# Joining float64 weights in two VectorE operations instead of three, and preparing the first weight earlier

## Chip, cores and metric

The kernel runs on one core of a Trainium2 chip. The metric is the device time of one execution in microseconds (us). Three executions of the kernel before took 1155.07, 1155.97 and 1156.25 us; the median is 1155.97 us.

## What is computed

Local attention, then a gated layer, then a second layer with SiLU; 3072 tokens, model width 512. All inputs arrive as float64 arrays for the weights and float32 for q, k and v (see `_layout`); the cut reference:

```python
# attention, chunks of 32 queries, window = 8 memory + 16 left + 32 + 8 right keys
scores = scale * q_c @ k_full.T
a = softmax(scores);  out[:, :, c] = a @ v_full
x = out.transpose(0, 2, 1, 3).reshape(3072, 512)
# first layer, d_ff 1536
x = (sigmoid(x @ w_gate) * (x @ w_val)) @ w_out
# second layer, d_ff 2048
h = x @ w_in
return (h * sigmoid(h)) @ w_out2
```

The weights are float64 on the device, seen as pairs of int32 words (low, high). The kernel makes a float32 of each, then splits that into two parts, a rounded one ("high part", fp32r) and the rest ("lower part"), and replaces each product by three matmuls: high x high, high x lower, lower x high.

## The kernel before

All engines run in an order written out by hand (`tc.manual_schedule()`); each engine takes its instructions in the order in which the program emits them, and waits where an input is not there.

**A weight unit** (class `Unit`, lines 96 to 135) is 128x512 float64 values, 512 KB, in a staging buffer `stg` (4 buffers). Its life has five steps: `load` (one DMA on SP's queue), `rebias` (ScalarE, L106: the high words, read as float32, times 2^-112, which moves the exponent's bias from double to single), `join` (VectorE, three operations: L114 shifts the low word right by 29, L117 ors the sign bit of the high word into it, L121 shifts the high word left by 3 and ors the low word to it, which gives the float32 `t`), `high` (ScalarE, L128: copy to fp32r), `rest` (VectorE, L131: `t` minus the high part). The class `Feed` moves three units at once: step k emits high of unit k-2, rebias of k, join of k-1, rest of k-2, and loads up to unit k+3.

**The first layer** takes the tokens in six blocks of 512 (index 0 to 5). In each block it goes over 12 slices f of the hidden width. A slice is 12 matmuls into `pg` (gate, L270), 12 into `pv` (value, L270) and 12 of the output product `y` of the slice before (L89, L91, L93), all 128x128 by 128x512. `pg` and `pv` share two PSUM banks, so the next `pv` waits until VectorE has multiplied this one (L285). After `pg` comes ScalarE's sigmoid (L280). In block 0 the three units of a slice are prepared on the way, one step of the feed after `pg`, one after `pv`, one after `y`: 36 units in all. In blocks 1 to 5 the first layer's weights are there, and the 32 units of the second layer pass through the same `rebias` and `join` (`prepare2`). The attention of the next block's four tiles of 128 tokens lies between: scores (L196, L209 to L211), normalising (L217 to L220), turning (L226, L227), product with v (L236, transposed by VectorE at L243).

**The start** (lines 400 to 431) computes the attention of block 0, four tiles in a pipeline, with idle transposes on TensorE (`warm`, L390). Unit 0 (the gate weight of slice 0) is rebiased and joined in the fifth round, its high part and the rebias of unit 1 (the value weight) are in the sixth. After the last tile's product, `split_x` makes the high and lower part of the four 128-row pieces of x (L81 on ScalarE, L84 on VectorE, or on GpSimd for the last NP pieces), then come the join of unit 1 and the rest of unit 0. The first `pg` of block 0 goes first over high and lower part of the weight with the high parts of x, and takes the four lower parts of x last; other slices of block 0 take the lower part of the weight last.

**The second layer** runs behind the first on prepared weights and its lines (L674, L787) are not touched.

Of the kernel before, what the change touches and what calls it, by code (L numbers as in the profile page):

```python
# [11 lines left out]
AF = mybir.ActivationFunctionType  # L12
ALU = mybir.AluOpType
# [21 lines left out]
LV = 1  # L35
NQ = ()
NJ = 8
NP = 2
NRING = 5

A11, S2, S1, S3, A12, A22, S4, A21 = range(8)
# [5 lines left out]
def moe_kernel(ctx: ExitStack, tc: tile.TileContext, qh, kh, vh, wg, wv, wo, w2i, w2o, out):  # L47
    nc = tc.nc
# [17 lines left out]
    def t_slot(name):  # L66
        return p1.tile([P, 512], F32, tag="t", name=name, bufs=2)
# [28 lines left out]
    class Unit:  # L96
# [5 lines left out]
            nc.sync.dma_start(out=self.stg.rearrange("p a b -> p (a b)"), in_=self.src)  # L102

        def rebias(self):
            high = self.stg[:, :, 1].bitcast(F32)
            nc.scalar.activation(out=high, in_=high, func=AF.Copy, scale=2.0**-112)  # L106

        def join(self, into=None):

            if into is None:  # L110
                self.t = t_slot(f"t_{self.name}")
                into = self.t
            low, high = self.stg[:, :, 0], self.stg[:, :, 1]
            nc.vector.tensor_scalar(  # L114
                out=low, in0=low, scalar1=29, scalar2=None, op0=ALU.logical_shift_right
            )
            nc.vector.scalar_tensor_tensor(  # L117
                out=low, in0=high, scalar=-2147483648, in1=low,
                op0=ALU.bitwise_and, op1=ALU.bitwise_or,
            )  # L120
            nc.vector.scalar_tensor_tensor(  # L121
                out=into.bitcast(I32), in0=high, scalar=3, in1=low,
                op0=ALU.logical_shift_left, op1=ALU.bitwise_or,
            )
# [63 lines left out]
    def att_scores(t, ps_sc, e):  # L188
        sc = ps_sc(f"sc{t}")
        scv = sc.rearrange("p (c2 a k) -> p c2 a k", c2=2, a=4)  # L190
        qb, kt = q_t.pop(t), k_t.pop(t)
        for c2 in range(2):
            for a in range(4):
                for cp in range(2):
                    c = 2 * c2 + cp
                    nc.tensor.matmul(  # L196
                        scv[cp * 64 : cp * 64 + 64, c2, a],
                        qb[:, 4 * a + c].rearrange("p u q -> p (u q)"),
                        kt[:, a, c],
                        start=True,  # L200
                        stop=True,
                    )
        if t % TPB == 0:
            nc.vector.memset(scv[0:64, 0, :, NMEM : NMEM + LEFT], NEG)
        if t % TPB == TPB - 1:
            nc.vector.memset(scv[64:128, 1, :, WIN - RIGHT : WIN], NEG)
        s3 = sc.rearrange("p (g k) -> p g k", k=WIN)
        m = att.tile([P, 8, 1], F32, tag="m", name=f"m{t}", bufs=2)
        nc.vector.tensor_reduce(m, s3, axis=AX.X, op=ALU.max)  # L209
        nc.vector.tensor_tensor(out=e, in0=s3, in1=m.to_broadcast([P, 8, WIN]), op=ALU.subtract)  # L210
        nc.scalar.activation(out=e, in_=e, func=AF.Exp, scale=SCALE)  # L211
        e_t[t] = e

    def att_norm(t, eng=nc.vector):
        e = e_t[t]
        r = att.tile([P, 8, 1], F32, tag="r", name=f"r{t}", bufs=2)
        nc.vector.tensor_reduce(r, e, axis=AX.X, op=ALU.add)  # L217
        nc.vector.tensor_scalar_add(r, r, 1e-9)
        nc.vector.reciprocal(r, r)
        eng.tensor_tensor(out=e, in0=e, in1=r.to_broadcast([P, 8, WIN]), op=ALU.mult)  # L220

    def att_turn(t, ps_pt, at):
        e = e_t.pop(t).rearrange("p g k -> p (g k)")
        pt = ps_pt(f"pt{t}")
        for i in range(4):
            nc.tensor.transpose(pt[:, i * P : (i + 1) * P], e[:, i * P : (i + 1) * P], ident)  # L226
        nc.scalar.copy(at.rearrange("p a b q -> p (a b q)"), pt)  # L227
        at_t[t] = at

    def att_pv(t, ps_px, xt, off):  # L230
        at, vb = at_t.pop(t), v_t.pop(t)
        px = ps_px(f"px{t}")
        for c in range(4):
            for j in range(4):
                q0 = 64 * (c % 2) + 32 * (j % 2)
                nc.tensor.matmul(  # L236
                    px[32 * j : 32 * j + 32, c * P : (c + 1) * P],
                    at[:, c // 2, j // 2, q0 : q0 + 32],
                    vb[c * len(vb) // 4][:, :, c % (4 // len(vb)), j],
                    start=True,  # L240
                    stop=True,
                )
        nc.vector.transpose(  # L243
            out=xt[:, :, off : off + P].rearrange("p k (c q) -> p c k q", c=4),
            in_=px.rearrange("p (c k q) -> p c k q", c=4, k=4),
        )
# [8 lines left out]
    def split_x(src, n, name, on_pool=0, hi_dve=()):  # L255
        xs = []
        for kt in range(KT):
            x = p1.tile([P, 2, 512], F32R, tag="x", name=f"{name}_{kt}", bufs=5)
            lo_eng = nc.gpsimd if kt >= KT - on_pool else nc.vector
            hi_eng = nc.vector if kt in hi_dve else nc.scalar  # L260
            split(x[:, 0, :n], x[:, 1, :n], src[:, kt, :n], lo_eng, hi_eng)
            xs.append(x)
        return xs
# [34 lines left out]
    with tc.manual_schedule():  # L298
# [57 lines left out]
        units = []  # L356
# [31 lines left out]
        def idle(n):  # L388
            for _ in range(n):
                nc.tensor.transpose(warm[:, :P], ident, ident)  # L390

        def prefetch(t):
            if t < NTILE:
                att_load_qk(t, qA, k_tile(t))

        def prefetch_v(t):
            if t < NTILE:
                att_load_v(t, vA)

        idle(22)  # L400
        for i in range(n0 + 2):
            if i < n0:
                att_scores(i, ps_y, es[i])
                idle(NI)
            if 0 <= i - 2 < n0:
                at = hold[0].tile([P, 512], F32, tag="sg", name=f"at{i - 2}", bufs=3)
                att_turn(i - 2, ps_a, at.rearrange("p (a b q) -> p a b q", a=2, b=2))
                idle(NI if i < 4 else 0)
            if 0 <= i - 1 < n0:
                att_norm(i - 1, nc.gpsimd if i - 1 in NQ else nc.vector)  # L410
            if 0 <= i - 3:
                att_pv(i - 3, ps_y, x32[0], (i - 3) * P)
                idle(NI if i < 4 else 0)
            if i == 1:
                prefetch(n0)
            if i == 4:
                prefetch_v(n0)
            if i == n0:
                units[0].rebias()
                units[0].join()  # L420
            if i == n0 + 1:
                units[0].high()
                units[1].rebias()
        att_pv(n0 - 1, ps_y, x32[0], (n0 - 1) * P)
        idle(NJ)
        x = split_x(x32.pop(0), BLOCKS1[0], "x0", NP, NH)
        units[1].join()
        units[0].rest()
        units[2].rebias()
        feed1.n = 3  # L430
        feed1.step()
# [525 lines left out]
```

## Time and profile before

| | |
|---|---|
| median of 3 runs (lowest, highest) | 1155.97 us (1155.07, 1156.25) |
| profiled execution: span, first to last instruction | 1153.2 us |
| what lies around the span, taken against the median | 2.8 us |
| TensorE matmul busy | 1133.1 us, 98% |
| VectorE busy | 685.9 us, 59%, 1013 instructions |
| ScalarE busy | 487.8 us, 42%, 708 instructions |
| GpSimd busy | 52.1 us, 5% |
| mean granted TensorE clock | 0.997 |

For the profiled execution the page gives the span and no other time; the 2.8 us is the median of the runs less the span. Starts are counted from the span's first instruction. A line of a timeline is one instruction, or several merged ones (x4). "Idle before" and the releaser behind an arrow say how long an engine had stood, and what ended it.

### The profile page before, as it was taken

Reading aid. Unit: us, or ns where it says so; the run is one execution under the profiler, and the core shown is the slowest. Engines: PE = TensorE matmul, PEld = TensorE weight load, DVE = VectorE, ACT = ScalarE, POOL = GpSimd, SP = SyncE. Lnnn points to the kernel's source line nnn. Section 1 sums busy time; section 2 is a strip of 40 time slices with the busy share of each in tenths; the row PEclk is TensorE's granted clock in tenths of the full one; section 3 lists DMA queues with packets and bytes.
Section 4 is the critical chain, followed back from the end, with each engine's and each line's share of the span. In section 5 each row is a group of like instructions: output and inputs, shape, how many; then the busy total and the mean of one; then the engine's idle time right before and its main releaser. Section 6 shows DMA issues by size and latency. Waiting matters only on the chain.

```text
span 1153.2 us, 15956 instructions
## 1 busy us (share of the span) xinstructions
PE 1133.1 (98%) x6319; PEld 926.5 (80%) x6319; DVE 685.9 (59%) x1013; ACT 487.8 (42%) x708; POOL 52.1 (5%) x46
## 2 busy tenths in 40 slices
PE   8899999999999999999999999999999999999998
PEld 6677788888888888888888888888888888888887
DVE  7899975455546555554545533348944379544665
ACT  3555643343334333433433324444434455344442
POOL 1000000000000000000000001111001110011000
PEclk9899999999999999999999999999999999999999
DMA  9787776667666566576565455575665575655552
GB/s 312 236 262 269 255 273 211 210 217 230 196 209 226 202 218 225 197 247 204 193 230 181 124 191 175 196 277 209 221 218 195 209 277 211 226 193 205 200 209 84
DMA packets 79210, 248.51 MB, mean 215 GB/s; under 512 B 7584, under 2 KB 23968, under 8 KB 69920
## 3 DMA queue, kind: packets, MB, share of 16 engines
q1 hardware_dynamic: 79136, 247.49, 63.2%
q8 instruction: 50, 0.82, 0.3%
q14 instruction: 24, 0.20, 0.1%
HBM read 199.23 MB, written 48.23 MB: 215 GB/s over the span
## 4 chain that ended last, share of the span: by engine, by line
PE 86%; DVE 9%; DMA 3%; issue 1%; ACT 1%; SPq 0%; DVEq 0%; ACTq 0%
PE o L787 20%; PE c L674 20%; PE pg L270 14%; PE pv L270 14%; PE y L89 5%; PE y L91 5%; PE y L93 5%; PE sc L196 2%; PE px L236 1%; DVE w L131 1%; DMA v<-in_vh_dram 1%; DVE stg_wv L117 1%; DVE sg L285 1%; PE pt L226 1%; DVE stg_wo L117 1%
## 5 line engine op out<-in xcount | busy, mean ns | idle before, releaser
L674 PE MATMUL c<-xp,wr 128*128 128x512 f32 x1008 | 229.1, 389 | 0.0
L787 PE MATMUL o<-gf,wr 128*128 128x512 f32 x1008 | 229.0, 389 | 0.0
L674 PEld LDWEIGHTS c<-xp,wr 128*128 128x128 f32 x1008 | 189.2, 188 | 39.3
L787 PEld LDWEIGHTS o<-gf,wr 128*128 128x128 f32 x1008 | 189.2, 188 | 39.3
L270 PE MATMUL pg<-x,w 128*128 128x512 f32 x864 | 211.8, 394 | 5.7 <-DVE w L131 5.2
L270 PE MATMUL pv<-x,w 128*128 128x512 f32 x864 | 211.2, 393 | 5.2 <-DVE sg L285 5.2
L270 PEld LDWEIGHTS pg<-x,w 128*128 128x128 f32 x864 | 162.3, 189 | 41.1 <-DVE w L131 5.6
L270 PEld LDWEIGHTS pv<-x,w 128*128 128x128 f32 x864 | 160.0, 188 | 41.9 <-issue 8.6
L84 DVE TENSOR_TENSOR gf<-g,gf 128x1024 fp32r<-128x1024 f32 x84 | 104.1, 1242 | 49.8 <-ACT gf L81 49.6
L81 ACT CAST gf<-g 128x1024 fp32r<-128x1024 f32 x84 | 88.3, 1055 | 86.7 <-PE o L787 71.4
L287 ACT CAST g<-sg 128x512 fp32r<-128x512 f32 x72 | 44.9, 623 | 156.1 <-DVE sg L285 156.1
L694 POOL TENSOR_TENSOR s<-s,s 128x512 f32<-128x512 f32 x24 | 36.0, 1498 | 943.6 <-ACT s L693 943.6
L290 DVE TENSOR_TENSOR g<-sg,g 128x512 fp32r<-128x512 f32 x72 | 49.8, 691 | 42.6 <-ACT g L287 42.6
L280 ACT ACTIVATE sg<-pg 128x512 f32<-128x512 f32 x72 | 43.0, 597 | 75.2 <-PE pg L270 62.0
L646 DVE TENSOR_TENSOR s<-c,s 128x512 f32<-128x512 f32 x48 | 33.2, 692 | 65.1 <-PE c L674 63.0
L89 PE MATMUL y<-g,wor 128*128 128x512 f32 x240 | 66.2, 397 | 0.5 <-DVE y L548 0.5
L91 PE MATMUL y<-g,wor 128*128 128x512 f32 x240 | 64.3, 390 | 0.0
L93 PE MATMUL y<-g,wor 128*128 128x512 f32 x240 | 64.1, 389 | 0.0
L285 DVE TENSOR_TENSOR sg<-pv,sg 128x512 f32<-128x512 f32 x72 | 49.4, 686 | 20.6 <-PE pv L270 20.5
L649 DVE TENSOR_TENSOR g<-g,g 128x1024 f32<-128x1024 f32 x48 | 58.6, 1220 | 0.0
L652 ACT ACTIVATE g<-s 128x512 f32<-128x512 f32 x48 | 30.4, 634 | 54.1 <-DVE s L646 54.1
L91 PEld LDWEIGHTS y<-g,wor 128*128 128x128 f32 x240 | 45.1, 188 | 9.6
(119 smaller groups left out, 1040.9 us busy)
## 6 DMA issues: line engine op xcount, KB each, us to landing
wr<-w2o_d SPq DMA_DIRECT2D x42, 1024.0 KB, 4.8
wor<-wo_d SPq DMA_DIRECT2D x60, 512.0 KB, 4.9
wr<-w2i_d SPq DMA_DIRECT2D x24, 1024.0 KB, 5.1
wr<-w2i_d SPq DMA_DIRECT2D x24, 768.0 KB, 4.4
w2o_d<-coo SPq DMA_DIRECT2D x56, 256.0 KB, 3.0
w2i_d<-coi SPq DMA_DIRECT2D x24, 512.0 KB, 3.0
qA<-in_qh_dram SPq DMA_DIRECT2D x21, 512.0 KB, 5.0
k<-in_kh_dram SPq DMA_DIRECT2D x21, 512.0 KB, 5.8
```

The lines of the kernel that those rows point to most:

```text
L81: nc.scalar.copy(hi, src)
L84: lo_eng.tensor_tensor(out=lo, in0=src, in1=hi.bitcast(F32), op=ALU.subtract)
L89: nc.tensor.matmul(o, w_hi, x_hi, start=first, stop=False)
L91: nc.tensor.matmul(o, w_hi, x_lo, start=False, stop=False)
L93: nc.tensor.matmul(o, w_lo, x_hi, start=False, stop=last)
L270: nc.tensor.matmul(o[:, :n], w[:, pw, kt * P : (kt + 1) * P], x[kt][:, px, :n], start=i == 0, stop=i == len(steps) - 1,)
L285: nc.vector.tensor_tensor(out=sg[:, :n], in0=psv[:, :n], in1=sg[:, :n], op=ALU.mult)
L287: nc.scalar.copy(g[:, 0, :n], sg[:, :n])
L290: nc.vector.tensor_tensor(out=g[:, 1, :n], in0=sg[:, :n], in1=g[:, 0, :n].bitcast(F32), op=ALU.subtract)
L649: nc.vector.tensor_tensor(out=o, in0=a, in1=b_, op=ALU.subtract)
L674: nc.tensor.matmul(o, w[:, pw, i % 4, kt * P : (kt + 1) * P], X[i][:, px, kt], start=first and j == 0, stop=j == 5, skip_group_check=not f ...
L787: nc.tensor.matmul(c[at[i], dp], w[:, pw, pl, dp * P : (dp + 1) * P], f[:, px, pl], start=i in (A11, S1, S2) and pp == 0 and j == 0, stop= ...
```

## The change

`rebias` uses the parametric ReLU with alpha 2^32 instead of a scaled copy. A positive word is multiplied by 2^-112 as before; a negative one by 2^-112 and 2^32. That adds 32 to the exponent field of negative words, which sets a bit that the shift by 3 in `join` carries to the sign position (the old sign bit is shifted out). So the operation that placed the sign (L117) is gone from `join`. NP goes from 2 to 0: GpSimd makes no lower part of x any more, VectorE makes all four. And in the sixth round of the start `rest` of unit 0 and `join` of unit 1 are emitted directly behind the rebias of unit 1, ahead of the last tile's product and `split_x`.

```diff
-NP = 2
+NP = 0
...
         def rebias(self):
+
             high = self.stg[:, :, 1].bitcast(F32)
-            nc.scalar.activation(out=high, in_=high, func=AF.Copy, scale=2.0**-112)
+            nc.scalar.activation(
+                out=high, in_=high, func=AF.Prelu, scale=2.0**-112, alpha=2.0**32
+            )
...
             nc.vector.tensor_scalar(
                 out=low, in0=low, scalar1=29, scalar2=None, op0=ALU.logical_shift_right
-            )
-            nc.vector.scalar_tensor_tensor(
-                out=low, in0=high, scalar=-2147483648, in1=low,
-                op0=ALU.bitwise_and, op1=ALU.bitwise_or,
             )
             nc.vector.scalar_tensor_tensor(
                 out=into.bitcast(I32), in0=high, scalar=3, in1=low,
...
             if i == n0 + 1:
                 units[0].high()
                 units[1].rebias()
+                units[0].rest()
+                units[1].join()
         att_pv(n0 - 1, ps_y, x32[0], (n0 - 1) * P)
         idle(NJ)
         x = split_x(x32.pop(0), BLOCKS1[0], "x0", NP, NH)
-        units[1].join()
-        units[0].rest()
         units[2].rebias()
```

## Rows read from the trace of the kernel before

**Rows 1.** The page's first section: busy time, share of the span, instructions.
```profile
PE 1133.1 (98%) x6319; PEld 926.5 (80%) x6319; DVE 685.9 (59%) x1013; ACT 487.8 (42%) x708; POOL 52.1 (5%) x46
```

**Rows 2.** Busy time by stage: length, PE, PEld, DVE, ACT, POOL, clock, DMA share, GB/s.
```profile
42.00:141.00 99.00, 92.74 (x594) 73.02 (x593) 94.18 (x167) 59.24 (x95) 0.00 (x0) 1.00 0.77 261
141.00:586.00 445.00, 445.00 (x2866) 361.05 (x2865) 245.23 (x443) 177.96 (x271) 0.00 (x0) 1.00 0.65 215
```

**Rows 3.** Waits of TensorE, whole span, then after 141 us: total, times, longest.
```profile
PE pg L270 <- DVE w L131: 5.2, 1, 5.2
PE pv L270 <- DVE sg L285: 5.2, 4, 2.1
...
PE y L89 <- DVE y L548: 0.5, 1, 0.5
```

**Rows 4.** Starts of slices 1 and 11: block 0 (timeline), block 1 (chain that ended last).
```profile
40.47 2.97 PE L270 MATMUL pg<-x,w 128*128 128x512 f32 x12
141.40 2.88 PE L270 MATMUL pg<-x,w 128*128 128x512 f32 x12
...
159.12 2.72 PE pg L270 x12
251.53 2.72 PE pg L270 x12
```

**Rows 5.** The chain that ended last, inside block 0: start, us, what.
```profile
75.70 0.71 DVE stg_wg L117
```

**Rows 6.** Timeline of the start: start, us, engine, line, operation, idle before.
```profile
23.94 0.69 DVE L117 SCALAR_TENSOR_TENSOR stg_wg<-stg_wg 128x512 int32<-128x512 int32 x1 [0.31 <-ACT stg_wg L106]
24.67 0.69 DVE L121 SCALAR_TENSOR_TENSOR t_wg<-stg_wg 128x512 int32<-128x512 int32 x1
25.28 1.43 DVE L243 STREAM_TRANSPOSE x<-px 128x512 f32<-128x512 f32 x2
25.39 0.62 ACT L128 CAST w<-t_wg 128x512 fp32r<-128x512 f32 x1 [1.02 <-DVE t_wg L121]
25.86 1.09 PE L390 MATMUL warm<-ident 128*128 128x128 f32 x8
26.22 0.68 ACT L106 ACTIVATE stg_wv<-stg_wv 128x512 f32<-128x512 f32 x1 [0.20 <-DMA stg_wv<-in_wv_dram]
26.80 2.17 ACT L81 CAST x<-x 128x512 fp32r<-128x512 f32 x4
27.44 1.29 DVE L84 TENSOR_TENSOR x<-x,x 128x512 fp32r<-128x512 f32 x2 [0.74 <-ACT x L81]
28.59 2.68 POOL L84 TENSOR_TENSOR x<-x,x 128x512 fp32r<-128x512 f32 x2 [22.85 <-ACT x L81]
...
30.18 1.64 DVE L117 SCALAR_TENSOR_TENSOR stg_wv<-stg_wv 128x512 int32<-128x512 int32 x1
33.20 4.67 PE L270 MATMUL pg<-x,w 128*128 128x512 f32 x11 [5.24 <-DVE w L131]
37.72 2.92 PE L270 MATMUL pv<-x,w 128*128 128x512 f32 x12
37.96 1.28 ACT L280 ACT_TABLE_LOAD   x1 [4.17 <-PE pg L270]
```

**Rows 7.** Busy time by stage, one stretch of the gap before the first slice.
```profile
30.50:31.00 0.50, 0.00 (x0) 0.00 (x0) 0.50 (x1) 0.00 (x0) 0.50 (x1) 0.50 0.98 213
```

**Rows 8.** Instruction groups, 42 to 141 us; last the whole span: busy, mean ns, idle.
```profile
L106 ACT ACTIVATE stg_wv<-stg_wv 128x512 f32<-128x512 f32 x10 | 6.8, 681 | 0.0
L280 ACT ACT_TABLE_LOAD x4 | 5.1, 1283 | 0.1
...
L81 ACT CAST gf<-g 128x1024 fp32r<-128x1024 f32 x84 | 88.3, 1055 | 86.7 <-PE o L787 71.4 <-DVE g L649 15.2
L117 DVE SCALAR_TENSOR_TENSOR stg_w2o<-stg_w2o 128x512 int32<-128x512 int32 x16 | 11.1, 696 | 7.2 <-ACT stg_w2o L106 6.1
```

**Rows 9.** The tile stg_wo, 18 to 50 us: its loads' time from issue to landing.
```profile
DMA to landing us min/median/max: 4.2/7.3/10.4
```

## The prediction

> **What bounds the kernel now.** The page's first section comes first: TensorE is busy 98% of the span [rows 1], so only stretches in which it stands or is slowed can give anything. The table by stage shows where: from 141 us on through blocks 1 to 4 TensorE is busy without a gap and VectorE little over half the time; in block 0, 42 to 141 us, TensorE lacks 6.3 us and VectorE is busy 94.18 of 99.00 us [rows 2]. TensorE's waits say the same: 5.2 us once, for the lower part of the first weight, 5.2 us in four pieces for the multiplication that frees the bank of `pv`, and after 141 us one wait of 0.5 us [rows 3]. A wait is not the whole loss, since the stream also has to fill again after it, so I measure block 0 by its pace: slices 1 to 11 take 141.40 - 40.47 = 100.93 us there and 251.53 - 159.12 = 92.41 us in block 1, with the same matmuls and the same four attention tiles at the same places [rows 4]. Block 0 loses 8.52 us. The chain of waits runs through VectorE's `join` in this block, where L117 is one link after another [rows 5].
>
> **Parts of the change, block 0.** L117 takes 0.71 us of the chain [rows 5]; three units a slice make 2.1 us less on VectorE. A slice there lasts 10.09 us on average (100.93 / 10), so VectorE's need, 94.18 / 99.00 of it or 9.6 us, falls to 7.5 us, below the 9.24 us of block 1's slices. VectorE ceases to set the pace and TensorE does: -8.52 us. What is late next? ScalarE needs 59.24 / 99.00 of 10.09 us, 6.0 us a slice [rows 2], of which three rebiases take 3 x 0.68 [rows 8]; it fits in 9.24 us. A load is asked for three feed steps, one slice, after its buffer comes free; loads land in 4.2 to 10.4 us [rows 9], so the slow ones can be late against 9.24 us. I keep 1.2 us of waits, nearer to none than to 8.52, since block 0 moved 261 GB/s in a DMA share of 0.77 [rows 2] and would need 0.77 x 100.93 / 92.41 = 0.84.
>
> **Prelu for the scaled copy.** The trace has no Prelu. The copy takes 0.681 us on 512 strided float32 [rows 8]. From below I take nothing away, since the same elements pass; from above 1.055 us, the cost of twice as many elements [rows 8], which would put ScalarE at 6.0 + 3 x 0.37 = 7.1 us a slice, still hidden. I take 0.68, the same engine on the same tile. Even the upper end costs about 0.4 us, at the rebias of unit 1 on the start's path.
>
> In blocks 1 to 5, 32 operations of 0.696 us [rows 8] leave VectorE: 22 us, worth nothing, as TensorE waits there only 0.5 us [rows 3].
>
> **The start.** All of these rows are [rows 6]. Unit 0: the join's last operation now stands where L117 stood, at 23.94, so `t` is ready at 24.63 and not at 25.36. The transpose of tile 2 follows (to 25.3), the high part ends at 25.3, and `rest` of unit 0, which waited last, ends at about 26.0. Now `join` of unit 1: its load landed at 26.2, its rebias still ends at 26.90, its second operation then runs 26.94 to 27.63. Queued behind it on VectorE is the transpose of tile 3, which stood at 25.99 to 26.71 and now ends at 28.3; ScalarE's four high parts of x wait for it and begin at 28.35 and not at 26.80. So the move costs 1.55 us first. The first matmul comes 0.65 us later, at 29.0. The four high parts end 2.17 us after their start, at 30.5. The four lower parts, all on VectorE now (0.65 us each, 1.29 for two), follow from 29.0 and end near 31.5. Taking two pieces from GpSimd costs VectorE 1.3 us, but removes what happened beside it: while GpSimd worked at 28.59 to 31.27, L117 took 1.64 us for its usual 0.69. Eight matmuls go in pace with the high parts, the four with the lower parts of x come last, and `pg` is issued by 31.8. Before, eleven of its twelve waited until 33.20 for the lower part of the weight and `pv` followed at 37.72. Unit 1's high part: ScalarE is done with x at 30.5, with the rebias of unit 2 at 31.1, with this copy at 31.7: in time for `pv` at 31.8. After `pg` the table load, sigmoid and unit 2's copy let slice 1 go 40.47 - 37.96 = 2.5 us after the load's start; ScalarE comes to it at 32.3, after the rebias of unit 3, so slice 1 starts at 34.8. That is 5.67 us earlier than 40.47. By pieces: `pv` begins 5.9 us earlier, and 0.3 us are given back at slice 1.
>
> On SP's queue no load is moved by hand, but those of units 5 and 6 wait for buffers that come free earlier, so they start earlier. The load of unit 4, `stg_wo`, was issued at 25.73 and took the longest time of [rows 9], to 36.1; it lies behind the attention's loads, and ScalarE will now ask for it at about 34.7. The 1.4 us that it is late hold up the copies for slice 1's `pv`, and are most of the 1.2 us kept above.
>
> **Sum.** Against the profiled span of 1153.2: -5.67 - 8.52 + 1.2 = -13.0, span 1140.2 us. The median of the runs lies 2.8 us over the span, and that part is untouched: 1155.97 - 13.0 = 1143.0 us.
>
> **TensorE's clock.** It was granted at 0.50, the lower of its two levels (1.2 of 2.4 GHz), at 30.5 [rows 7], after TensorE had stood from 27.96 on (33.20 less 5.24 [rows 6]), and eleven matmuls then took 4.5 us. At the pace of block 1 (12 in 2.72 us [rows 4]) they would take 2.5. In the new order TensorE stands about 2.05 us, from the last `warm` transpose (25.86 + 1.09 = 26.95) to 29.0 [rows 6], and then works in pace with ScalarE. I take it that the clock stays up.
>
> **Rivals.** (1) The clock falls all the same: 2.0 us lost by the rows above, 1145.0 us. For it: eight of `pg`'s matmuls come only as fast as ScalarE delivers x. Against: the gap is shorter than the one of 2.5 us before the fall. (2) The feed's loads become the bound: each attention tile's loads stand in front of a weight's, and at the longest landing of 10.4 us against 9.24 us a slice, four tiles cost 4 x 1.2 = 5 us in place of the 1.2 kept, 1146.8 us. (3) Prelu is not in the table that Exp or Sigmoid loads. In block 0 eight loads of 1.283 us stand for four tiles (four of them in [rows 8]), and the copies between cause none. If Prelu needs its own table, each slice gets two more, one ahead of the rebiases and one ahead of the sigmoid: without its eight loads ScalarE's need is (59.24 - 10.3) / 9.8 = 5.0 us a slice, 7.6 with two, under 9.24; in the four slices that have an Exp with its own two it is 10.1, 0.9 us over. Four times that and one load at the start, 4.9 us: 1148 us.
> The Trainium skill, page "ScalarE: Activation LUTs", section "Table sets: the hidden batching unit", says that only cheap functions stand in every table set, and names relu, copy, identity and abs for it, not the parametric one; by it a switch of sets costs about 2.66 us with its drain. The load alone measures 1.283 us in this trace, as that page has it; whether Prelu is a filler no row here shows. By its price rival 3 would need 5.0 + 1.0 + 5.3 = 11.3 us a slice and be over the old pace, near 1163 us. The trace speaks against the drain: from the load at 37.96 to slice 1 at 40.47 there are 2.5 us, with a sigmoid and a copy in them.
> (4) Only the start gains, as some other wait holds block 0 at its old pace: 1155.97 - 5.67 = 1150.3 us. Against it: VectorE is the only releaser that the trace names in that block. (5) Slower than before: Prelu carries a table switch both ways for itself, as the copies to fp32r between the rebiases would call the other table back. A rebias is then 0.68 + 2 x 1.283 = 3.25 us, ScalarE needs 6.0 - 2.0 + 9.7 = 13.7 us a slice and becomes the bound; ten slices take 137 us where 100.93 stood, less the start's 5.67: 1187 us. It decides from a rebias of 2.2 us on, where 4.0 + 3 x 2.2 = 10.6 us a slice eats both the block's old pace and the start. Against it: the kernel before mixes Exp, Sigmoid and copies and pays loads only between the first two.
>
> **How the numbers follow.** Forecast 0.61, rival 1 0.12, rival 2 0.12, rival 3 0.05, rival 4 0.04, rival 5 0.04, no change 0.02. A measurement of this kernel tells 0.2%, 2.3 us, from no change; the cases up to rival 4 all lie beyond it. Faster 0.94, same 0.02, slower 0.04. If no wait is kept at all, the time is 1141.8; with a little for the start's reckoning the range begins at 1141. It ends at 1148, with rivals 1 to 3 inside.
>
> **What would show it.** The first `pg` beginning near 29.0 and slice 1 near 34.8; slices 1 to 11 of block 0 in about 93 us; no granted 0.50 there; 8 table loads in that block as before; ACT L106 near 0.68 us; TensorE waits on VectorE below 1 us in all. Wrong it is if ScalarE's waits for `stg` loads turn up as waits of `pv`, if more table loads appear, or if TensorE's first matmul is not within a microsecond of 29.0.

## The result, and the profile after

The changed kernel takes 1142.72 us (median of 4 runs, 1142.29 to 1144.26) where the kernel before takes 1156.11 on the same chip (4 runs): ratio 0.9888, 95% interval [0.9874, 0.9902]. That is 13.4 us less; 13.0 were forecast. The profiled execution has a span of 1140.3 us, 12.9 less than before. In a slower state of the chip one execution of e9_late_join below took 1615.12 us at a mean granted clock of 0.655, and it is left out of that run's median.

The timeline of the start of the changed kernel (start, us, engine, line, operation, idle before) answers to [rows 6]; line numbers above 107 have moved by a few.

```profile
25.80 0.54 SPq L102 DMA_DIRECT2D stg_wo<-in_wo_dram  x1
25.99 1.10 PE L389 MATMUL warm<-ident 128*128 128x128 f32 x8
26.34 0.71 ACT L107 ACTIVATE stg_wv<-stg_wv 128x512 f32<-128x512 f32 x1 [0.66 <-DMA stg_wv<-in_wv_dram]
27.08 0.69 DVE L120 SCALAR_TENSOR_TENSOR t_wv<-stg_wv 128x512 int32<-128x512 int32 x1 [0.31 <-ACT stg_wv L107]
27.69 0.71 DVE L242 STREAM_TRANSPOSE x<-px 128x512 f32<-128x512 f32 x1
28.43 2.18 ACT L81 CAST x<-x 128x512 fp32r<-128x512 f32 x4 [1.39 <-DVE x L242]
29.10 3.22 PE L269 MATMUL pg<-x,w 128*128 128x512 f32 x12 [2.02 <-ACT x L81]
32.16 2.90 PE L269 MATMUL pv<-x,w 128*128 128x512 f32 x12
32.41 1.28 ACT L279 ACT_TABLE_LOAD   x1
33.70 0.60 ACT L279 ACTIVATE sg<-pg 128x512 f32<-128x512 f32 x1
34.90 2.99 PE L269 MATMUL pg<-x,w 128*128 128x512 f32 x12
36.42 0.69 ACT L107 ACTIVATE stg_wo<-stg_wo 128x512 f32<-128x512 f32 x1 [1.61 <-DMA stg_wo<-in_wo_dram]
39.18 3.00 PE L269 MATMUL pv<-x,w 128*128 128x512 f32 x12 [0.22 <-DVE sg L284]
127.86 2.88 PE L269 MATMUL pg<-x,w 128*128 128x512 f32 x12
```

The join waits for the load of unit 1, the last tile's transpose for the join, ScalarE for the transpose and TensorE for ScalarE. But `pg` then runs through in one piece: slice 1 starts at 34.90 instead of 40.47, slice 11 (the last row) at 127.86 instead of 141.40 [rows 4].

The waits of TensorE over the whole span (total, times, longest), the table by stage (42 to 141 us: length, PE, PEld, DVE, ACT, POOL, clock, DMA share, GB/s) and two groups of ScalarE in this stretch, all of the changed kernel, answer to [rows 2, 3, 8].

```profile
PE pg L269 <- ACT x L81: 2.0, 1, 2.0
...
PE y L89 <- DVE y L547: 0.7, 1, 0.7
PE pt L225 <- DVE e L219: 0.4, 1, 0.4
PE pt L225 <- DVE e_w L219: 0.3, 1, 0.3
PE pv L269 <- DVE sg L284: 0.2, 1, 0.2
```
```profile
42.00:141.00 99.00, 99.00 (x630) 80.17 (x629) 81.73 (x148) 62.93 (x103) 0.00 (x0) 1.00 0.85 293
```
```profile
L107 ACT ACTIVATE stg_wv<-stg_wv 128x512 f32<-128x512 f32 x9 | 6.1, 677 | 0.3 <-DMA stg_wv<-in_wv_dram 0.3
L279 ACT ACT_TABLE_LOAD x4 | 5.1, 1283 | 0.1
```

Block 0's stretch is now full on TensorE (99.00 of 99.00 us), VectorE has fallen from 94.18 to 81.73, and of 5.2 us of waiting for the bank of `pv` 0.2 are left. Prelu costs 0.677 us, the copy 0.681; the page counts 21 table loads before Exp and 21 before Sigmoid, as before.

### The profile page after: what moved, and what is told of

Read it like the earlier page. It is cut to its first block, busy times and chain, and to the rows that moved or that the text cites. A ratio compares the mean times of both kernels' runs of the same rounds, so it can differ in the third digit from the quotient of the medians.

```text
span 1140.3 us, 15875 instructions
## 1 busy us (share of the span) xinstructions
PE 1128.1 (99%) x6319; PEld 924.6 (81%) x6319; DVE 640.3 (56%) x947; ACT 486.8 (43%) x708; POOL 49.4 (4%) x44
## 4 chain that ended last, share of the span: by engine, by line
PE 95%; DMA 4%; DVE 1%; SPq 0%; ACT 0%; issue 0%; DVEq 0%; ACTq 0%
PE o L786 20%; PE c L673 20%; PE pv L269 17%; PE pg L269 16%; PE y L89 6%; PE y L91 6%; PE y L93 6%; PE sc L195 2%; PE px L235 2%; DMA vA<-in_vh_dram 1%; DMA stg_wo<-in_wo_dram 1%; PE pt L225 1%; DMA stg_wg<-in_wg_dram 1%; DMA yd<-y 1%; DMA w2i_d<-coi 0%; DMA k<-in_kh_dram 0%
```

## Experiments

Each run is set against the kernel before on its own chip; "the full change" is the changed kernel. On the chips used, the medians of the kernel before lie between 1155.60 and 1156.31 us, so a difference of less than 1 us from the full change is not told by the times. A slice's pace is the start of slice 11 less that of slice 1 in block 0.

**e1_join.** Only `rebias` and `join` are changed; NP and the order are those of before.
```diff
-            nc.scalar.activation(out=high, in_=high, func=AF.Copy, scale=2.0**-112)
+            nc.scalar.activation(out=high, in_=high, func=AF.Prelu, scale=2.0**-112, alpha=2.0**32)
...
-            nc.vector.scalar_tensor_tensor(  # the sign, L117
```


> The join in two operations with Prelu, alone; start and NP as before. My theory: block 0's slices go at TensorE's pace, about 8 us gained there (slices 1 to 11 in about 93 us), and the start gains only the removed operation, 0.65 us; TensorE still stands for the lower part of the first weight until about 32.5 us and the clock still falls. Time near 1147.5 us. Rival (only the start gains, block 0 is held by something else): 1155.4 us, slices 1 to 11 in 100 us.

1146.9 us, ratio 0.9922 [0.9905, 0.9938]. The starts of slices 1 and 11 in its timeline:
```profile
40.76 2.98 PE L268 MATMUL pg<-x,w 128*128 128x512 f32 x12
133.28 2.88 PE L268 MATMUL pg<-x,w 128*128 128x512 f32 x12
```
Slices 1 to 11 take 133.28 - 40.76 = 92.52 us. TensorE still waits 4.5 us once for the lower part of the first weight, and its clock is at 0.50 at 33 us. So the pace of block 0 was VectorE's, and L117 made the difference (that Prelu itself costs what the copy did is shown by e5_copy). The start gained nothing: slice 1 comes at 40.76 for 40.47, where 0.65 us less was expected.

**e2_order.** The full change with the old `rebias` and the three operations of `join`.
```diff
+            nc.scalar.activation(out=high, in_=high, func=AF.Copy, scale=2.0**-112)
...
+            nc.vector.scalar_tensor_tensor(  # the sign, as before
```


> The new order of the start and NP = 0, alone, with the scaled copy and the join in three operations. My theory: the start gains 4 to 5 us, a little less than in the full change, since two more operations of 0.73 us stand before the last tile's transpose (first pg near 29.9, slice 1 near 35.8), the granted clock stays up; VectorE still sets block 0's pace at about 100 us for slices 1 to 11. Time near 1151.4 us. Rival (the pace of block 0 was lost by the late start and not by VectorE's work): block 0 recovers too, 1144 us.

1152.48 us, ratio 0.9973 [0.9961, 0.9984]: 3.1 us and not 4 to 5. The same two starts:
```profile
37.48 3.01 PE L271 MATMUL pg<-x,w 128*128 128x512 f32 x12
138.48 2.89 PE L271 MATMUL pg<-x,w 128*128 128x512 f32 x12
```
Slices 1 to 11 take 138.48 - 37.48 = 101.00 us, so the rival falls. Slice 1 starts at 37.48, not 35.8: the first `pg` comes at 30.36, TensorE has stood 3.3 us, and its clock does fall (0.57 in the stretches 30 to 32 and 32 to 34 us). The two parts alone give 8.7 + 3.1 = 11.8 us; together 13.4. The intervals of the three ratios are too wide to establish these 1.6 us, but the traces show them in the start: against 40.47, slice 1 comes 0.3 us later in e1_join, 3.0 earlier here and 5.6 earlier in the full change. The short join also makes the early order pay, since it lets the last transpose go sooner (first `pg` at 29.10 for 30.36).

**e3_np0.** The kernel before with NP = 0.
```diff
-NP = 2
+NP = 0
```


> NP = 0 alone: VectorE makes all four lower parts of x, everything else as before. My theory: VectorE has 1.3 us more to do but the two operations of the join that ran beside GpSimd go back from 1.5 and 1.64 us to 0.43 and 0.69, so the lower part of the first weight is there about 0.7 us earlier; 1155.4 us, not told from no change. Rival (what GpSimd did was free and VectorE's extra work is on the path): 1157.4 us.

1155.36 us, ratio 0.9996 [0.9987, 1.0005]: no difference, as expected. Its timeline of VectorE shows the trade:
```profile
27.98 2.50 DVE L84 TENSOR_TENSOR x<-x,x 128x512 fp32r<-128x512 f32 x4 [0.74 <-ACT x L81]
30.40 0.42 DVE L114 TENSOR_SCALAR stg_wv<-stg_wv 128x512 int32<-128x512 int32 x1
30.86 0.69 DVE L117 SCALAR_TENSOR_TENSOR stg_wv<-stg_wv 128x512 int32<-128x512 int32 x1
```
Four lower parts instead of two, and the two operations behind them back at 0.42 and 0.69 us, of which the second took 1.64 beside GpSimd [rows 6]. `pg` goes on at 32.93 for 33.20, 0.3 us earlier where 0.7 was expected.

**e4_np2.** The reverse: the full change with NP = 2.
```diff
-NP = 0
+NP = 2
```


> The full change with NP = 2: GpSimd makes the last two lower parts of x. My theory: pg of slice 0 ends about 1 us later, near 33, since GpSimd's pieces take 1.36 us each, but slice 1's pv is held by the load of unit 4 anyway and loses about 0.5 us: 1143.2 us. Rival (NP = 0 carries the start's gain): 2 us or more slower.

1142.75 us, ratio 0.9884 [0.9869, 0.9899]; the full change's own median is 1142.72, so NP tells nothing in the time, though slice 1 starts 1.4 us later in this profile (36.27) and slice 2 1.1 us (45.84; 0.5 was expected). In its timeline the slow pair is back, and `pg` waits for GpSimd:
```profile
30.42 2.72 POOL L84 TENSOR_TENSOR x<-x,x 128x512 fp32r<-128x512 f32 x2 [24.68 <-ACT x L81]
30.47 1.54 DVE L117 TENSOR_SCALAR stg_wg<-stg_wg 128x512 int32<-128x512 int32 x1
32.12 1.57 DVE L120 SCALAR_TENSOR_TENSOR t_wg<-stg_wg 128x512 int32<-128x512 int32 x1
33.20 0.50 PE L269 MATMUL pg<-x,w 128*128 128x512 f32 x1 [0.91 <-POOL x L84]
```
The Trainium skill, page "SBUF — State Buffer", section "SBUF: two separate sides", calls the port pair of the two engines "an exclusive lock, not a bandwidth split". The rows agree in kind: the two VectorE operations take 1.1 and 0.9 us more than alone, a little less than one GpSimd operation of 1.36 us each.

**e5_copy.** The full change with the scaled copy for Prelu; the sign of negative weights is left out of the computation.
```diff
-                out=high, in_=high, func=AF.Prelu, scale=2.0**-112, alpha=2.0**32
+                out=high, in_=high, func=AF.Copy, scale=2.0**-112
```


> The full change with the scaled copy in place of Prelu, so the sign of negative weights is left out of the join. My theory: Prelu costs what the copy costs, 0.68 us each, and no table load; the same time as the full change, 1142.7 us. Rival (Prelu is dearer or brings table loads that block 0 hides only partly): 1 us or more faster than the full change, fewer than 43 table loads.

1142.83 us, ratio 0.9886 [0.9871, 0.9901], and 43 table loads in both. Prelu shows no extra cost.

**e6_act1 and e6_act3.** The full change with one, or three, copies by 1.0 over the high words ahead of each rebias from unit 3 on.
```diff
             if k < len(u):
+                for _ in range(1):     # 3 in e6_act3
+                    u[k].again()       # activation(out=high, in_=high, func=AF.Copy, scale=1.0)
                 u[k].rebias()
```


> The full change with one more ScalarE pass over the high words (a copy by 1.0) ahead of each rebias from unit 3 on: a rebias then costs 1.36 us. My theory: ScalarE's need in block 0 goes from 5.9 to about 7.9 us a slice, still under TensorE's 9.3: no more than 0.5 us slower than the full change, 1142.7 to 1143.2 us. Rival (ScalarE's order is already on the path in block 0): each pass shows, 5 us slower or more.

> The full change with three more such passes: a rebias costs 2.72 us. By the prediction's rival 5 ScalarE needs 4.0 + 3 x 2.72 = 12.2 us a slice and sets the pace: slices 1 to 11 in about 121 us where 93 stood, about 1172 us, slower than the kernel before. Rival (ScalarE runs ahead enough to hide it): below 1156 us.

One pass: 1143.27 us, ratio 0.9889 [0.9871, 0.9906], not told from the full change. The table by stage (42 to 141 us) has ScalarE busy 83.05 of 99 us:
```profile
42.00:141.00 99.00, 98.82 (x628) 79.77 (x628) 82.55 (x149) 83.05 (x132) 0.00 (x0) 1.00 0.82 287
```
Slices 1 to 11 take 129.51 - 36.28 = 93.23 us, 0.3 more than in the full change. Three passes: 1174.27 us, ratio 1.0156 [1.014, 1.0172]. There ScalarE is the bound, as the table by stage (42 to 141 us), TensorE's waits and the starts of slices 1 and 11 show:
```profile
42.00:141.00 99.00, 81.31 (x533) 62.12 (x533) 62.84 (x114) 96.51 (x153) 0.00 (x0) 1.00 0.68 222
```
```profile
PE pv L275 <- DVE sg L290: 12.3, 10, 2.8
PE pg L275 <- ACT w L131: 10.5, 7, 2.2
```
```profile
37.85 4.40 PE L275 MATMUL pg<-x,w 128*128 128x512 f32 x12 [1.85 <-ACT w L131]
159.08 3.04 PE L275 MATMUL pg<-x,w 128*128 128x512 f32 x12 [1.13 <-ACT w L131]
```
Slices 1 to 11 take 159.08 - 37.85 = 121.23 us, 12.1 a slice; 12.2 were worked out. The waits on VectorE are ScalarE's too: its multiplication stands behind joins that wait for rebiases. So the mechanism of rival 5, a dearer rebias, is real; Prelu is only far from it.

**e8_table.** The full change with a tiny Exp once a slice in block 0, which calls the other table.
```diff
             self.load(k + 1)
+            if k % 3 == 1:
+                nc.scalar.activation(out=spare, in_=spare, func=AF.Exp, scale=SCALE)   # 128x8
```


> The full change with one tiny Exp a slice in block 0 and behind it (one per three feed steps), so that a table load comes before the slice's rebiases and another before its sigmoid, as if Prelu needed a table of its own. By the prediction's rival 3: 4.9 us slower than the full change, 1147.6 us. By a switch price of 2.66 us: ScalarE over TensorE's pace in every slice, 1156 us or more. If ScalarE's cover is as wide as its busy share says: 1143 us.

1147.67 us, ratio 0.9929 [0.9913, 0.9944]: 4.95 us over the full change, 4.9 worked out. Its groups of table loads in 42 to 141 us are 11, 9 and 2, where the full change has 8:
```profile
L282 ACT ACT_TABLE_LOAD x11 | 14.1, 1283 | 0.2
L155 ACT ACT_TABLE_LOAD x9 | 11.5, 1283 | 0.2
...
L213 ACT ACT_TABLE_LOAD x2 | 2.6, 1283 | 0.0
```
That is one load ahead of each sigmoid and one ahead of an Exp, two a slice, since the tiny Exp and the attention's Exp share a load. The four slices with four loads, which made 3.6 of the 4.9 us of rival 3, do not occur here. By the rival's own reckoning ScalarE would need 5.0 + 2 x 1.283 + 0.2 = 7.8 us a slice, under TensorE's pace, and only the load at the start, 1.3 us, would show. So the agreement in the total is chance. In the trace slices 1 to 11 take 134.32 - 38.45 = 95.87 us, 2.9 over the full change, with 2.1 us of waits for the bank of `pv`, although ScalarE is busy only 80.49 of 99 us, less than in e6_act1. The forecast that its cover is as wide as its busy share says, 1143 us, fails: it counts where a load stands. At the start `pg` of slice 1 waits 1.3 us for ScalarE's copy behind one more load. The profiled execution is the slowest of its four (1149.43 us), and TensorE's clock was low at its start as well (0.50 from 27 to 33 us). The price of 2.66 us a switch in the Trainium skill (page "ScalarE: Activation LUTs", section "What ACT_TABLE_LOAD costs") does not hold here: a load shows 1.283 us, ScalarE stands 0.4 us in all before these 22, and in the timeline of the start above the sigmoid begins 0.01 us behind the load.

**e9_late_join, e10_loads, e11_both.** The full change with the join of unit 1 behind the last tile's product; with the load of unit 4 ahead of the next attention tile's; with both.
```diff
                 units[1].rebias()
+                feed1.load(5)          # e10, e11; the prefetches of rounds 1 and 4 go here
+                prefetch(n0)
+                prefetch_v(n0)
                 units[0].rest()
-                units[1].join()        # e9, e11
         att_pv(n0 - 1, ps_y, x32[0], (n0 - 1) * P)
+        units[1].join()
```


> The full change, but the join of unit 1 is emitted behind the last tile's product, so the transpose of tile 3 no longer waits for the load and rebias of unit 1. My theory: the first pg comes about 1.2 us earlier (27.8 to 28.0), slice 1 near 33.8, but slice 1's pv still waits for the load of unit 4 that lands near 36.3 and starts near 39.2: same time as the full change, 1142.7 us. Rival (the start's order sets the end, as the prediction's sum has it): 1.2 us faster, 1141.5 us.

> The full change, but the load of unit 4 is issued ahead of the loads of the next attention tile. My theory: it lands near 31 instead of 36.3 and slice 1's pv no longer waits for VectorE behind it; it can then start near 38.95 instead of 39.18: about 0.2 us, 1142.5 us, not told from the full change by time but by the wait that is gone. Rival (the feed's loads hold more than this wait): 1 us faster or more.

> Both of these: later join of unit 1 and earlier load of unit 4. My theory: only together they shorten the start, slice 1's pv near 37.8 instead of 39.2, 1141.3 us. Rival (the two add up from what each does alone): as the sum of the two runs beside it.

e9: 1142.23 us, ratio 0.988 [0.9863, 0.9896]; the times can't tell 1142.7 from 1141.5, the trace can. The first `pg` comes at 27.71 and slice 1 at 33.66, 1.2 us earlier; then slice 1's `pv` waits until 39.58 (timeline):
```profile
33.66 2.93 PE L269 MATMUL pg<-x,w 128*128 128x512 f32 x12
39.58 3.00 PE L269 MATMUL pv<-x,w 128*128 128x512 f32 x12 [1.91 <-DVE sg L284]
```
ScalarE had stood 3.3 us for `stg_wo`: what the order gains, the load takes. e10: 1143.47 us, ratio 0.9887 [0.987, 0.9903]. ScalarE no longer waits for `stg_wo`, but the clock fell in its profiled execution, as the table by stage from 30 to 31 us shows for the full change and then for e10:
```profile
30.00:31.00 1.00, 1.00 (x5) 0.59 (x4) 1.00 (x3) 1.00 (x3) 0.00 (x0) 1.00 1.12 258
```
```profile
30.00:31.00 1.00, 1.00 (x4) 0.71 (x4) 1.00 (x3) 1.00 (x3) 0.00 (x0) 0.50 1.03 406
```
From `pg` at 29.19 to `pv` at 33.62 are 4.43 us, where the full change has 3.06, and the load's 0.2 us can't be read from that. e11: 1141.83 us, ratio 0.9878 [0.9863, 0.9893]. Slice 2 starts at 43.23 against 44.74 in the full change and 45.14 in e9, the span is 1138.6, 1.7 us less than the full change's; the medians differ by 0.9 us and the intervals overlap, so a gain is in the trace and not established by the times.

**e12_warm.** The full change with more idle transposes up to the first slice.
```diff
-NJ = 8
+NJ = 22
```


> The full change with 22 in place of 8 idle transposes ahead of the first slice (NJ = 22), so that TensorE has work until about 28.9 us. My theory: the clock can fall for some 3.4 us after the gap of 2.05 us, in some executions and not in others (first slice to value product 3.1 us at the upper level, 4.4 us at the lower one); with the gap filled it never falls, the profile shows 1.00 throughout and the runs lie together near 1142.4 us. Rival (the spread of the runs has another cause): the range stays at 1.5 us or more, or the clock falls again.

1142.48 us, ratio 0.9876 [0.986, 0.9893]. The clock stays at 1.00 in the profile, but the runs still spread from 1141.35 to 1143.26 us: the rival holds. In its profile `stg_wo` came late, ScalarE's rebias of it began at 37.84 (36.42 in the full change), and slice 1's `pv` waited 1.3 us. The landing of this load may be a part of the spread, but that is not shown: e11_both, where the load comes earlier and ScalarE does not wait for it in the profiled execution, spreads from 1140.63 to 1143.50 us at a mean granted clock of 1.000 in all four executions. The cause of the spread stays open.

## Why the prediction was right

| step | forecast | full change |
|---|---|---|
| first `pg`, us | 29.0 | 29.10 |
| `pv` of slice 0 | 31.8 | 32.16 |
| slice 1 | 34.8 | 34.90 |
| slices 1 to 11 (92.41 + 1.2 kept) | 93.6 | 92.96 |
| given back behind block 0 | 0 | 0.61 |
| change of the span | -13.0 | -12.9 |

**The start.** Every link came within 0.4 us: the transpose held back by the join, the sum for `pg`, the load and copy ahead of slice 1. NP alone is worth nothing that the times show (e3_np0, e4_np2): taking GpSimd's pieces costs VectorE about what it frees.

**Block 0.** VectorE's L117 was the term (e1_join: 92.52 us without it, e2_order: 101.00 with it), and ScalarE had the room that its busy share said for a dearer rebias: 1.36 us each are hidden (e6_act1), 2.72 are not, and then a slice takes the 4.0 + 3R of the prediction, R being the rebias (e6_act3). For table loads that reckoning fails (e8_table). The operations that leave VectorE in blocks 1 to 5 are worth nothing, as forecast: all starts of slices in blocks 1 and 2 that the traces show whole are the same 13.54 us earlier.

**The 1.2 us kept was mis-sized.** The cause was right: `stg_wo` lay at the end of its queue and ScalarE stood 1.61 us for it, 1.4 forecast. By the prediction's last sentence such a wait turning up at `pv` is a sign of being wrong, and it does turn up. But between it and `pv` there is slack, the attention's scores lie in front of that `pv`, so only 0.22 us show as its wait and 92.96 - 92.41 = 0.55 us in the pace. Against that stand 0.61 us that the sum did not have. Slice 11 of block 0 is 13.54 us earlier than before, the end only 12.93. In block 3 a turn waits 0.4 us for VectorE and in block 5 a `y` waits 0.7 where 0.5 stood [rows 3]. Behind the first is a store on the one buffer `coi`; ScalarE's row at that place, kernel before, then the changed one:
```profile
440.25 0.62 ACT L81 CAST coi<-fi 128x512 fp32r<-128x512 f32 x1 [2.96 <-DMA w2i_d<-coi]
```
```profile
427.10 0.62 ACT L81 CAST coi<-fi 128x512 fp32r<-128x512 f32 x1 [3.42 <-DMA w2i_d<-coi]
```
It waits 0.46 us longer, VectorE stands behind it, and TensorE's turn waits in the changed kernel, where before it did not:
```profile
430.36 0.63 PE L225 MATMUL pt<-ident,e 128*128 128x128 f32 x4 [0.38 <-DVE e L219]
```
The two errors cancel; that the total came out within 0.3 us is partly luck. TensorE's waits on VectorE come to 1.6 us in all in the changed kernel (0.3 of it at an attention tile of the start, as before), where below 1 us was forecast.

**The 2.8 us around the span.** This was the median of the runs less the span of one execution, and that was one of the shortest. Taken run by run, 1.7 to 1.8 us lie around the span in the 15 executions of the kernel before beside e1_join, and 2.0 to 2.1 us in the changed kernel. The rest of the 2.8 is spread between executions. Only the difference of two spans went into the forecast, so the error does not show; it is also a part of why the medians differ by 13.4 us and the profiled spans by 12.9.

**The clock.** "I take it that the clock stays up" held in the profiled execution and not in all: with the same gap of 2.0 us it fell in those of e5_copy, e6_act1 and e10_loads and not in that of e4_np2. Where it fell, `pg` to `pv` takes 4.4 us for 3.1, 1.3 to 1.4 us more and not the 2.0 of rival 1, and slice 2 starts 1.2 us later (45.96, 45.91 and 45.93 for 44.74), since the full change spends part of the difference waiting for `stg_wo`. In e5_copy the two executions with a mean granted clock of 0.998 took 1143.06 and 1143.14 us, the two with 1.000 took 1142.01 and 1142.60. How often it falls was not measured beyond that.

**The rivals.** Table loads (3): its condition is not met, 43 as before (e5_copy); its price is not tested, since e8_table meets it by chance. The feed (2): the load of `stg_wo` is late, and one later load costs ScalarE 0.3 us and TensorE no wait. Only the start (4): refuted by e1_join. Slower (5): its condition is not met. A rebias of 2.72 us does make the kernel slower and one of 1.36 does not; the threshold of 2.2 lies between and was not located.

## What to carry to other kernels

Where one engine is the bound of only one stage, measure that stage's pace against a later stage with the same work: the difference, here 8.5 us, is what relieving the engine is worth, and the same operation removed elsewhere in this kernel is worth nothing. Before moving work ahead, follow the next input that each consumer needs: e9_late_join moved the first matmul 1.4 us forward, and a load issued behind others took it back. Parts of a change need not add up: the start of slice 1 came 0.3 us later with one part, 3.0 earlier with the other, and 5.6 earlier with both. A total that agrees with the forecast does not show that its terms do: look at the terms, as with the 1.2 us here and with e8_table.

## What the runs showed of the hardware

Prelu with an immediate alpha costs the same as a scaled copy on 512 strided float32 (0.677 and 0.681 us) and adds no table load between Exp and Sigmoid. TensorE's clock can fall or not after the same gap of 2.0 us in different executions of nearly the same start (0.50 from 30 to 32 us in e10_loads, 1.00 in the full change). The same happened inside block 0: after a wait of 2.1 us at the same `pv` it stood at 0.50 from 86 to 89 us in e3_np0 and at 1.00 in the kernel before.
